# Moving part of the pattern adds of an attention kernel from VectorE to GpSimd

## The chip, the cores and the metric

The kernel runs on one core of a Trainium2 chip. The metric is the device time of one execution in microseconds (us), the median of several runs. Executions of one kernel agree within some 0.3 per cent, apart from a slower state in some executions, at a lower granted TensorE clock (the share of full speed that PE was allowed); comparisons use fast runs alone. The core has five engines that work side by side and wait for each other by semaphores: PE (TensorE, matmuls), ACT (ScalarE, here the exponentials), DVE (VectorE), POOL (GpSimd) and SP, which issues transfers.

## The reference

Self-attention over 2048 positions, width 448, 16 heads of 28, in bf16:

```python
qkv = (x @ wqkv).reshape(B, S, 3, H, Dh).transpose(2, 0, 3, 1, 4)
scores = einsum("bhqd,bhkd->bhqk", q, k) * Dh ** -0.5
o = einsum("bhqk,bhkd->bhqd", softmax(scores), v)
out = o.transpose(0, 2, 1, 3).reshape(B, S, D) @ wo
```

## The kernel before

The 16 units of work (four groups of four heads, four chunks of 512 queries) each have 16 key tiles, so 256 key tiles of four heads. For most tiles ScalarE takes the exponential straight from PSUM, two banks at a time. For the rest, called batches, VectorE makes it another way: it turns a score into an int16 whose bits, read as fp16, approximate the exponential. Three patterns that differ by a constant (0, 341, 683) are used, and PE sums their three products. So a batch costs VectorE four reads of PSUM (one for each head) and two adds in SBUF over all four heads, and PE three passes in place of one:

```python
D_COUNT = (4, 5, 6, 3, 5, 6, 4, 6, 4, 4, 5, 5, 5, 4, 6, 3)   # batches in each unit: 75
TERM_D = (0, 341, 683)
...
r = P.add("dve", ... e.tensor_scalar(PD[:, zs, 0, h * 512:(h + 1) * 512], bank(...), ZBIAS, 0.0, ALU.add, ALU.max) ...)
...                                       # after the fourth head:
h1 = P.add("dve", ... e.tensor_scalar(PD[:, zs, 1, :], PD[:, zs, 0, :], float(TERM_D[1]), None, ALU.add) ...)
h2 = P.add("dve", ... e.tensor_scalar(PD[:, zs, 2, :], PD[:, zs, 0, :], float(TERM_D[2]), None, ALU.add) ...)
```

`P.add` records an operation with an estimate of its duration. A scheduler in the kernel places all of them by these estimates, and what reaches the chip is **one fixed order for each engine**, with semaphores for the true dependencies. Nothing is reordered afterwards: an operation that is late holds all that stands behind it on its engine.

Of the kernel before, what the change touches and what calls it, by code (L numbers as in the profile page):

```python
# [7 lines left out]
ALU = mybir.AluOpType  # L8
# [10 lines left out]
class _Op:  # L19
    __slots__ = ("eng", "emit", "deps", "after", "dur", "prio", "name", "idx", "sig", "count",  # L20
                 "t0", "t1", "dma_group", "dma_index", "acq", "rel", "banks", "slack", "nbytes", "relpool", "acq_slack", "kind", "units", "heads", "ride", "hold", "fill", "lock", "fill_unit")

    def __init__(self, eng, emit, deps, after, dur, prio, name, idx, dma_group):
# [27 lines left out]
        self.lock = False  # L51

# [10 lines left out]
class _Prog:  # L63

    SYNC_LAT = 135.0
    LAT = {"pe": 230.0, "act": 192.0, "dve": 135.0, "pool": 140.0}
# [5 lines left out]
    HOLD_BACK = 540.0  # L72
    BIGLOOK = 150.0
# [28 lines left out]
    def pe_dur(self, prev, op, t):  # L102

        if op.kind is None:
            return op.dur
        one, switch = (430.0, 110.0) if t < self.COLD_UNTIL else (218.0, 100.0)
        if prev is None or prev.kind != op.kind:
            return switch + one * op.units
        if op.kind == "r" and op.heads and not set(op.heads) & self.burst:
            return 60.0  # L110
        return one * op.units

    def schedule(self):
        ops = self.ops
        n = len(ops)
# [18 lines left out]
        def start_of(i, ft):  # L134
# [8 lines left out]
            if op.lock:  # L143
                st = max(st, self.lock_free)
            if op.hold is not None and op.hold.t0 is not None:
# [149 lines left out]
D_COUNT = (4, 5, 6, 3, 5, 6, 4, 6, 4, 4, 5, 5, 5, 4, 6, 3)  # L295
# [38 lines left out]
def _fast(nc, x, wqkv, wo, out, n_heads=16):  # L334
# [35 lines left out]
    with es:  # L370
# [38 lines left out]
        P.pool("M", [4, 5, 6, 7])  # L409
# [135 lines left out]
        def proj_v(g, c, prio):  # L545
# [3 lines left out]
            for j in range(4):  # L549
# [8 lines left out]
                mms.append((f, [dma_x[c], dma_w[(2, 1 if g else 0)]] + wdep(c), "f", 1.1))  # L558
# [6 lines left out]
            for k in range(2):  # L565
# [3 lines left out]
                           deps=[ev, ms_v1], after=[sc], dur=345, prio=g * 4 + c - 2.0, name=f"vb{g}_{c}_{k}")  # L569
                v_ev[(g, c)].append(sc)  # L570
            src = VX[:, xs, :].rearrange("p (n h d) -> p n h d", n=4, d=DH)[:, j0:4:js, :, :]
            for j in range(NTERM):
                dst = VC[:, s0:s0 + nb, j, g * 128:(g + 1) * 128].rearrange("p n (h r) -> p n h r", r=32)[:, :, :, 0:DH]
                sc = P.add("pool", (lambda e, dst=dst, j=j: e.tensor_scalar(dst, src, TERM_C[j], 1.0, ALU.mult, ALU.mult)),  # L574
                           deps=[ev, ms_c1[j]], after=[sc], dur=350, prio=g * 4 + c, name=f"vc{g}_{c}_{j}")
            vc_ev[(g, c)] = sc
# [36 lines left out]
        while i < NA:  # L613
            w = 2
            groups.append(list(range(i, min(i + w, NA))))
            i += w
# [4 lines left out]
        LEAD = 4  # L621
        NMP = 4
        RIDE = 12000.0
# [51 lines left out]
        def out_proj(n, pr, eng):  # L675
# [3 lines left out]
            for gg in range(G):  # L679
                def f_op(e, gg=gg):  # L680
# [3 lines left out]
                            after=[prev], kind="f", units=0.9, prio=pr if gg == 0 else min(pr, -4.0), name=f"OP{n}_{gg}", acq=(("M", 1) if gg == 0 else None), slack=3000.0 if gg == 0 else 0.0)  # L684
# [16 lines left out]
        PRE_LEAD = -0.20  # L701
        s_tail = []
        op_last = []

        def post_unit(u):
# [22 lines left out]
            for k in range(NMP):  # L728
# [3 lines left out]
                           deps=[l4], after=[nm], dur=400, prio=pr + 0.2, name=f"NM{u}_{k}")  # L732
            ots_last[ub] = nm
# [5 lines left out]
        def tail():  # L739
# [7 lines left out]
            b_l, b_p = (0, 2)[nl % 2], (0, 2)[(nl - 1) % 2]  # L747
# [3 lines left out]
            def pbank(j):  # L751
                return heads_[j].banks[0] if j < NQT - 1 else b_p
            for j in range(NQT):
                n = c * NQT + j
                op = None
                for gg in range(G - 1):
                    def f_pre(e, j=j, n=n, gg=gg):
# [3 lines left out]
                    op = P.add("pe", f_pre, deps=[otn_ev[(gg, c)]] + dma_wo[-1:] + ([bank_last[b_p]] if first and j == NQT - 1 else []),  # L761
                               after=([last_s[0]] if first and j == NQT - 1 else sd_of[u][-4:] + op_last[-4:]) if first else [op],
                               kind="f", units=0.9, prio=(NU - PRE_LEAD if gg < 2 else T) + 0.1 * j + 0.01 * gg, name=f"PREOP{j}_{gg}", acq=("M", 1) if first and j < NQT - 1 else None)
# [8 lines left out]
            N1B = (b_p + 1, b_l)  # L772
            N2B = (b_l + 1, b_p + 1)
# [11 lines left out]
            for k in range(2):  # L785
# [14 lines left out]
                for j in (2 * k, 2 * k + 1):  # L800
# [5 lines left out]
                    if j % 2 == 0:  # L806
                        ev = P.add("act", (lambda e, j=j: e.activation(OUTS[:, j, :], bank(pbank(j))[:, 0:D], AF.Identity)), deps=[fin, outs_last[j]], dur=540,
                                   prio=-50.0 + j, name=f"OPEV{n}", rel=[(heads_[j], 0)] if j < NQT - 1 else [])
                    else:
                        ev = P.add("dve", (lambda e, j=j: e.tensor_copy(OUTS[:, j, :], bank(pbank(j))[:, 0:D])), deps=[fin, outs_last[j]], dur=600,  # L810
                                   prio=-50.0 + j, name=f"OPEV{n}", rel=[(heads_[j], 0)] if j < NQT - 1 else [])
# [74 lines left out]
        z_tiles = {}  # L886

# [23 lines left out]
        for gi, gr in enumerate(groups):  # L911
            tl = [a_tiles[a] for a in gr]
            w = len(tl)
            b0 = (0, 2)[gi % 2]
# [15 lines left out]
            s = P.add("pe", f_s, deps=deps, after=[last_s[0]], kind="r", units=1.0, heads=tuple(h for _, _, h in tl), prio=-1000.0 + pos, name=f"S{gi}")  # L930
            last_s[0] = s
            s.hold = last_exp[0]
            while release and release[0][0] - 0.06 <= pos:
                release.pop(0)[1].after.append(s)
            ex = P.add("act", (lambda e, p0=p0, w=w, b0=b0: e.activation(PT[:, p0 * 512:(p0 + w) * 512], bank(b0, w), AF.Exp, scale=ESCALE)),  # L935
                       deps=[s] + [pt_last.get(p0 + j) for j in range(w)], after=[last_exp[0]], dur=51 + w * 427, prio=pos, name=f"E{gi}")
# [9 lines left out]
            for (bi, h) in d_at[gi]:  # L946
# [3 lines left out]
                sd = P.add("pe", (lambda e, hold=hold, u=u, kt=kt, h=h: s_one(e, hold[0].banks[0], u, kt, h)), deps=s_deps(u, kt), after=[s],  # L950
                           kind="r", units=1.0, heads=(h,), prio=-1000.0 + pos + 0.0001, name=f"SD{bi}_{h}", acq=("M", 1))
# [4 lines left out]
                          deps=[sd, z_last[zs][0]], dur=600, prio=-90.0, name=f"R{bi}_{h}", rel=[(sd, 0)])  # L956
                z_tiles.setdefault(bi, []).append(r)
                if len(z_tiles[bi]) == 4:
# [4 lines left out]
                    h2 = P.add("dve", (lambda e, zs=zs: e.tensor_scalar(PD[:, zs, 2, :], PD[:, zs, 0, :], float(TERM_D[2]), None, ALU.add)),  # L963
                               deps=rs_ + [z_last[zs][2]], after=[h1], dur=600, prio=pos, name=f"H{bi}_2")
                    evs += [[h1], [h2]]

                    def mk(u=u, kt=kt, zs=zs, evs=evs):
# [3 lines left out]
                        z_last[zs][0] = op  # L971
# [17 lines left out]
        ckb = (0, 2)[(len(groups) - 1) % 2]  # L989
# [728 lines left out]
```

## Time and profile before

| | before |
|---|---|
| median | 355.8 us |
| span of the profiled run | 353.3 us |
| exponentials on ScalarE | 362, 332.4 us busy, 1.3 us idle before them |
| VectorE busy | 328.9 us |
| GpSimd busy | 68.4 us |

"Busy" is the time in which at least one instruction of an engine was open. Idle time just before a group of instructions is given with the instruction that ended it. The lines are shown in the prediction below.

One more view: GpSimd in the order of time. Columns are the start, the length, the engine, source line, operation, output and input, their forms, and how many followed each other; in brackets the idle time before and its releaser.

```profile
13.35 0.72 POOL L568 TENSOR_SCALAR V<-VX 128x224 bf16<-128x224 f32 x2 [6.26 <-DVE VX L517]
14.03 0.88 POOL L574 TENSOR_SCALAR VC<-VX 128x112 bf16<-128x112 f32 x3
16.09 1.09 POOL L568 TENSOR_SCALAR V<-VX 128x224 bf16<-128x224 f32 x2 [1.18 <-DVE VX L517]
```

The view calls these copies TENSOR_SCALAR.

### The profile page before, as it was taken

The page shows a single profiled execution, that of the slowest core. Times are in us where ns is not written, and L with a number is a line of the kernel's source. Part 1 is how long each engine was busy: PE and PEld are TensorE (multiplying, and loading weights), DVE is VectorE, ACT ScalarE, POOL GpSimd, SP SyncE. Part 2 cuts the span into 40 slices and gives each one's busy share as a digit, 9 for nine tenths or more (in the row PEclk, how much of TensorE's full clock was granted, in tenths as well). Part 3 has the DMA queues.
Part 4 walks back from the last instruction along what each step waited for, and adds up shares of the span by engine and source line. Part 5 has one row for each costly group of instructions (what it writes and reads, how often), then busy time and mean ns, then how long its engine had stood idle before and what let it go on. Part 6 is the DMA issues. An engine that isn't in the chain of part 4 may idle for free.

```text
span 353.3 us, 8533 instructions
## 1 busy us (share of the span) xinstructions
PE 332.5 (94%) x3601; PEld 97.5 (28%) x3601; DVE 328.9 (93%) x557; ACT 335.5 (95%) x367; POOL 68.4 (19%) x157
## 2 busy tenths in 40 slices
PE   7999999999999999999999999999999899999993
PEld 3333232223322222332322222223222222222231
DVE  1788999999999999999999999999999999999962
ACT  2999999999999999999999999999999999999971
POOL 7332030042043013104030121340120301010010
PEclk9999999999999999999999999999999999999999
DMA  9910010010100000010100101010000101020111
GB/s 186 216 24 2 15 39 2 5 32 2 32 19 18 0 5 32 0 34 3 33 2 4 33 1 33 3 33 2 13 21 5 32 30 58 16 71 13 42 34 59
DMA packets 21604, 10.63 MB, mean 30 GB/s; under 512 B 15676, under 2 KB 19516, under 8 KB 21560
## 3 DMA queue, kind: packets, MB, share of 16 engines
q1 hardware_dynamic: 20136, 9.71, 11.4%
q8 instruction: 30, 0.49, 0.6%
q10 hardware_dynamic: 1424, 0.31, 0.5%
q14 instruction: 14, 0.11, 0.1%
HBM read 5.83 MB, written 2.08 MB: 22 GB/s over the span
## 4 chain that ended last, share of the span: by engine, by line
ACT 87%; PE 7%; DVE 2%; DMA 2%; SPq 0%; issue 0%
ACT PT L935 87%; PE ps L846 3%; PE ps L894 2%; DMA xT<-in_x_dram 2%; DVE PD L961 1%; PE ps L758 1%; DVE PD L955 1%; DVE PD L963 1%; SPq L442 0%; PE ps L533 0%; PE ps L804 0%; PE ps L793 0%; PE ps L681 0%; PE ps L780 0%; DVE OUTS L810 0%
## 5 line engine op out<-in xcount | busy, mean ns | idle before, releaser
L935 ACT ACTIVATE PT<-ps 128x1024 bf16<-128x1024 f32 x362 | 332.4, 1252 | 1.3 <-PE ps L894 1.3
L955 DVE TENSOR_SCALAR PD<-ps 128x512 int16<-128x512 f32 x300 | 192.7, 682 | 7.8 <-PE ps L894 6.7
L894 PE MATMUL ps<-QT,KT 28*128 28x512 bf16 x1024 | 148.9, 384 | 11.1 <-ACT PT L935 9.5
L846 PE MATMUL ps<-PD,VC 128*32 128x512 f16 x900 | 80.0, 386 | 0.9 <-DVE PD L963 0.5
L894 PEld LDWEIGHTS ps<-QT,KT 28*128 28x128 bf16 x1024 | 37.9, 91 | 149.7 <-ACT PT L935 141.4
L846 PE MATMUL ps<-PT,V 128*32 128x512 bf16 x724 | 64.5, 385 | 0.7 <-DVE KT L517 0.2
L730 POOL TENSOR_TENSOR QT<-RB,OTS 128x128 bf16<-128x128 f32 x60 | 30.8, 544 | 161.7 <-DMA RB<-scr_r 161.5
L963 DVE TENSOR_SCALAR PD<-PD 128x2048 int16<-128x2048 int16 x75 | 53.5, 713 | 0.0
L961 DVE TENSOR_SCALAR PD<-PD 128x2048 int16<-128x2048 int16 x75 | 53.2, 709 | 0.1
L533 PE MATMUL ps<-xT,w_raw 128*32 128x512 bf16 x512 | 42.6, 385 | 1.4 <-DMA xT<-in_x_dram 0.6
L568 POOL TENSOR_SCALAR V<-VX 128x224 bf16<-128x224 f32 x32 | 12.6, 412 | 113.0 <-DVE VX L517 112.9
L846 PEld LDWEIGHTS ps<-PD,VC 128*32 128x32 bf16 x900 | 19.1, 94 | 32.6 <-issue 22.2
L846 PEld LDWEIGHTS ps<-PT,V 128*32 128x32 bf16 x724 | 15.7, 94 | 23.9 <-issue 20.7
L555 PE MATMUL ps<-w_raw,xT 128*128 128x112 bf16 x256 | 20.8, 215 | 0.0
L574 POOL TENSOR_SCALAR VC<-VX 128x112 bf16<-128x112 f32 (+1 forms) x48 | 19.0, 408 | 1.0
L555 PEld LDWEIGHTS ps<-w_raw,xT 128*128 128x128 bf16 x256 | 13.3, 98 | 10.9 <-issue 9.5
L533 PEld LDWEIGHTS ps<-xT,w_raw 128*32 128x32 bf16 x512 | 10.0, 94 | 19.5 <-issue 13.1
L681 PE MATMUL ps<-wop,QT 128*128 128x448 bf16 x48 | 13.5, 358 | 0.1
L517 DVE CAST KT<-ps 128x512 bf16<-128x512 f32 x16 | 11.0, 686 | 0.4 <-PE ps L533 0.3
L515 DVE TENSOR_SCALAR QT<-ps 128x512 bf16<-128x512 f32 x15 | 10.3, 685 | 0.3 <-PE ps L533 0.2
L713 DVE COPY OTS<-ps 128x512 f32<-128x512 f32 x15 | 10.3, 684 | 0.0
L517 DVE COPY VX<-ps 128x448 f32<-128x448 f32 x16 | 9.9, 618 | 0.3 <-PE ps L555 0.2
(50 smaller groups left out, 50.5 us busy)
## 6 DMA issues: line engine op xcount, KB each, us to landing
RB<-scr_r SPq DMA_DIRECT2D x60, 64.0 KB, 2.0
out_dram<-OUTS SPq DMA_DIRECT2D x16, 112.0 KB, 1.7
w_raw<-in_wqkv_dram SPq DMA_DIRECT2D x3, 249.0 KB, 4.3
wop<-in_wo_dram SPq DMA_DIRECT2D x16, 24.5 KB
w_raw<-in_wqkv_dram ACTq DMA_DIRECT2D x3, 87.0 KB, 3.9
scr_l<-OTS SPq DMA_DIRECT2D x15, 8.0 KB
LT<-scr_l SPq DMA_DIRECT2D x15, 8.0 KB, 1.6
scr_r<-RS SPq DMA_DIRECT2D x15, 8.0 KB, 1.4
```

The costliest lines, as they stand in the source:

```text
L517: fe = (lambda e: e.tensor_copy(evac[0](), evac[1](hold[0].banks[0])))
L533: ins = e.matmul(ps[32 * h:32 * h + 32, b * 512:(b + 1) * 512], w_raw[:, wi(c, it), col:col + 32], xT[:, it, c * 512:(c + 1) * 512], start ...
L555: ins = e.matmul(ps[:, b * 512 + j * GD:b * 512 + (j + 1) * GD], xT[:, it, n * 128:(n + 1) * 128], w_raw[:, wi(c, it), 2 * D + g * GD:2 * ...
L574: sc = P.add("pool", (lambda e, dst=dst, j=j: e.tensor_scalar(dst, src, TERM_C[j], 1.0, ALU.mult, ALU.mult)), deps=[ev, ms_c1[j]], after=[ ...
L681: return e.matmul(bank(hold[0].banks[0])[:, 0:D], QT[:, gg, n * 128:(n + 1) * 128], wop[:, gg, :], start=(gg == 0), stop=(gg == G - 1))
L730: nm = P.add("pool", (lambda e, k=k: e.tensor_tensor(QT[:, g, c * QCH + k * w_:c * QCH + (k + 1) * w_], RB[:, ub, k * w_:(k + 1) * w_], OT ...
L846: return e.matmul(ps[32 * h:32 * h + 32, accb(u) * 512:(accb(u) + 1) * 512], lhsT, rhs, start=first, stop=False, skip_group_check=True, ti ...
L894: return e.matmul(bank(b), KT[32 * h:32 * h + DH, g, kt * 128:(kt + 1) * 128], QT[32 * h:32 * h + DH, g, c * QCH:(c + 1) * QCH], start=Tru ...
L935: ex = P.add("act", (lambda e, p0=p0, w=w, b0=b0: e.activation(PT[:, p0 * 512:(p0 + w) * 512], bank(b0, w), AF.Exp, scale=ESCALE)), deps=[ ...
L955: r = P.add("dve", (lambda e, hold=hold, zs=zs, h=h: e.tensor_scalar(PD[:, zs, 0, h * 512:(h + 1) * 512], bank(hold[0].banks[0]), ZBIAS, 0 ...
L961: h1 = P.add("dve", (lambda e, zs=zs: e.tensor_scalar(PD[:, zs, 1, :], PD[:, zs, 0, :], float(TERM_D[1]), None, ALU.add)), deps=rs_ + [z_l ...
L963: h2 = P.add("dve", (lambda e, zs=zs: e.tensor_scalar(PD[:, zs, 2, :], PD[:, zs, 0, :], float(TERM_D[2]), None, ALU.add)), deps=rs_ + [z_l ...
```

## The change

VectorE and ScalarE both stand near 94 per cent, GpSimd at 19. For 72 per cent of the batches the second add goes to GpSimd, head by head as soon as the head's PSUM read is done. The scheduler is made to treat VectorE's adds in SBUF and GpSimd's work as excluding each other (point (1) of the prediction says why), so it gets a lock between them, and it starts a GpSimd piece together with a PSUM read on VectorE. The freed time is used for three more batches, so six fewer exponentials. The diff, cut to its core:

```diff
-D_COUNT = (4, 5, 6, 3, 5, 6, 4, 6, 4, 4, 5, 5, 5, 4, 6, 3)
+D_COUNT = (5, 4, 6, 6, 5, 4, 4, 4, 5, 5, 5, 5, 6, 5, 5, 4)
...
+            if op.pair and order["dve"]:
+                last = order["dve"][-1]
+                if last.t1 > st and (last.lock or st > last.t0 + self.PAIR_LATE):
+                    st = last.t1 + 1.0
...
-        LEAD = 4
+        LEAD = 18
...
+        POOL_SHARE = 72
+        GDUR = 590
...
+                if on_pool(bi):
+                    gp = z_pool.setdefault(bi, [])
+                    gp.append(P.add("pool", (lambda e, zs=zs, h=h: e.tensor_scalar(PD[:, zs, 2, h * 512:(h + 1) * 512], PD[:, zs, 0, h * 512:(h + 1) * 512],
+                                                                                  float(TERM_D[2]), 0.0, ALU.add, ALU.add)),
+                                    deps=[r, z_last[zs][2]], after=gp[-1:], dur=GDUR, prio=-90.0 + 0.001 * gi, name=f"G{bi}_{h}"))
+                    gp[-1].lock = True
+                    gp[-1].pair = True
```

The scheduler is told 590 ns for a piece (`GDUR`). Latencies, unit times, two more planning constants and the banks of the last unit are adjusted as well, and a PSUM read now waits for all three passes of the batch that had its buffer before (cut here).

More of the change, by code (lines that the diff above doesn't have):

```diff
@@ L20 @@
     __slots__ = ("eng", "emit", "deps", "after", "dur", "prio", "name", "idx", "sig", "count",
-                 "t0", "t1", "dma_group", "dma_index", "acq", "rel", "banks", "slack", "nbytes", "relpool", "acq_slack", "kind", "units", "heads", "ride", "hold", "fill", "lock", "fill_unit")
+                 "t0", "t1", "dma_group", "dma_index", "acq", "rel", "banks", "slack", "nbytes", "relpool", "acq_slack", "kind", "units", "heads", "ride", "hold", "fill", "lock", "pair", "fill_unit")
     def __init__(self, eng, emit, deps, after, dur, prio, name, idx, dma_group):
@@ L51, in __init__ @@
         self.lock = False
+        self.pair = False
 class _DmaGroup:
@@ L65 @@
     SYNC_LAT = 135.0
-    LAT = {"pe": 230.0, "act": 192.0, "dve": 135.0, "pool": 140.0}
+    LAT = {"pe": 225.0, "act": 185.0, "dve": 135.0, "pool": 140.0}
     SAME_LAT = 200.0
@@ L72 @@
     HOLD_BACK = 540.0
+    PAIR_LATE = 250.0
     BIGLOOK = 150.0
@@ L105, in pe_dur @@
             return op.dur
-        one, switch = (430.0, 110.0) if t < self.COLD_UNTIL else (218.0, 100.0)
+        one, switch = (430.0, 110.0) if t < self.COLD_UNTIL else (226.0, 100.0)
         if prev is None or prev.kind != op.kind:
@@ L109, in pe_dur @@
         if op.kind == "r" and op.heads and not set(op.heads) & self.burst:
-            return 60.0
+            return 8.0
         return one * op.units
@@ L407, in i32v @@
             return ap.bitcast(I32)
-        P.pool("M", [4, 5, 6, 7])
+        GW = (2, 2)
+        GB = (0, GW[0])
+        MB = list(range(sum(GW), 8))
+        P.pool("M", MB)
         ms_zw = P.add("pool", lambda e: e.memset(i32v(ZW[:, :]), 0), dur=120, prio=-20, name="ms_zw")
@@ L557, in f @@
                     return ins
-                mms.append((f, [dma_x[c], dma_w[(2, 1 if g else 0)]] + wdep(c), "f", 1.1))
+                mms.append((f, [dma_x[c], dma_w[(2, 1 if g else 0)]] + wdep(c), "f", 0.92))
             xs = vx_n[0] % 3
@@ L569, in proj_v @@
                            deps=[ev, ms_v1], after=[sc], dur=345, prio=g * 4 + c - 2.0, name=f"vb{g}_{c}_{k}")
+                sc.lock = True
                 v_ev[(g, c)].append(sc)
@@ L575, in proj_v @@
                            deps=[ev, ms_c1[j]], after=[sc], dur=350, prio=g * 4 + c, name=f"vc{g}_{c}_{j}")
+                sc.lock = True
             vc_ev[(g, c)] = sc
@@ L613, in _fast @@
         while i < NA:
-            w = 2
+            w = GW[len(groups) % 2]
             groups.append(list(range(i, min(i + w, NA))))
@@ L620, in _fast @@
                 g_of[a] = gi
-        LEAD = 4
+        LEAD = 18
         NMP = 4
-        RIDE = 12000.0
+        RIDE = 6000.0
         d_at = [[] for _ in groups]
@@ L683, in out_proj @@
                 opm = P.add("pe", f_op, deps=[otn_ev[(gg, cc)]] + (([otn_ev[(g_, cc)] for g_ in range(G)] + dma_wo[-1:]) if gg == 0 else []),
-                            after=[prev], kind="f", units=0.9, prio=pr if gg == 0 else min(pr, -4.0), name=f"OP{n}_{gg}", acq=(("M", 1) if gg == 0 else None), slack=3000.0 if gg == 0 else 0.0)
+                            after=[prev], kind="f", units=0.86, prio=pr if gg == 0 else min(pr, -4.0), name=f"OP{n}_{gg}", acq=(("M", 1) if gg == 0 else None), slack=3000.0 if gg == 0 else 0.0)
                 prev = opm
@@ L699, in out_proj @@
                                   nbytes=128 * D * 2)
-        PRE_LEAD = -0.20
+        PRE_LEAD = 0.00
         s_tail = []
+        ck_bank = []
         op_last = []
@@ L732, in post_unit @@
                            deps=[l4], after=[nm], dur=400, prio=pr + 0.2, name=f"NM{u}_{k}")
+                nm.lock = True
             ots_last[ub] = nm
@@ L746, in tail @@
             nl = len(groups) - 1
-            b_l, b_p = (0, 2)[nl % 2], (0, 2)[(nl - 1) % 2]
+            NPM = min(len(MB) - 1, NQT)
+            spare = [GB[(nl - 1) % 2] + i for i in range(GW[(nl - 1) % 2])] + [GB[nl % 2] + i for i in range(GW[nl % 2])]
+            pre_b = [spare.pop(0) for _ in range(NQT - NPM)]
+            N1B = (spare.pop(0), spare.pop(0))
+            N2B = (spare.pop(0), N1B[0])
+            ck_bank.append(N1B[1])
             pre = []
@@ L751, in pbank @@
             def pbank(j):
-                return heads_[j].banks[0] if j < NQT - 1 else b_p
+                return heads_[j].banks[0] if j < NPM else pre_b[j - NPM]
             for j in range(NQT):
@@ L760, in tail @@
                     first = gg == 0
-                    op = P.add("pe", f_pre, deps=[otn_ev[(gg, c)]] + dma_wo[-1:] + ([bank_last[b_p]] if first and j == NQT - 1 else []),
-                               after=([last_s[0]] if first and j == NQT - 1 else sd_of[u][-4:] + op_last[-4:]) if first else [op],
-                               kind="f", units=0.9, prio=(NU - PRE_LEAD if gg < 2 else T) + 0.1 * j + 0.01 * gg, name=f"PREOP{j}_{gg}", acq=("M", 1) if first and j < NQT - 1 else None)
+                    op = P.add("pe", f_pre, deps=[otn_ev[(gg, c)]] + dma_wo[-1:] + ([bank_last[pre_b[j - NPM]]] if first and j >= NPM else []),
+                               after=([last_s[0]] if first and j >= NPM else sd_of[u][-4:] + op_last[-4:]) if first else [op],
+                               kind="f", units=0.86, prio=(NU - PRE_LEAD if gg < 2 else T) + 0.1 * j + 0.01 * gg, name=f"PREOP{j}_{gg}", acq=("M", 1) if first and j < NPM else None)
                     if first:
@@ L771, in tail @@
                                 after=av[-1:], dur=340, prio=-95.0, name=f"ACCEV{u}_{k}"))
-            N1B = (b_p + 1, b_l)
-            N2B = (b_l + 1, b_p + 1)
             rs_h = []
@@ L807, in tail @@
                         ev = P.add("act", (lambda e, j=j: e.activation(OUTS[:, j, :], bank(pbank(j))[:, 0:D], AF.Identity)), deps=[fin, outs_last[j]], dur=540,
-                                   prio=-50.0 + j, name=f"OPEV{n}", rel=[(heads_[j], 0)] if j < NQT - 1 else [])
+                                   prio=-50.0 + j, name=f"OPEV{n}", rel=[(heads_[j], 0)] if j < NPM else [])
                     else:
                         ev = P.add("dve", (lambda e, j=j: e.tensor_copy(OUTS[:, j, :], bank(pbank(j))[:, 0:D])), deps=[fin, outs_last[j]], dur=600,
-                                   prio=-50.0 + j, name=f"OPEV{n}", rel=[(heads_[j], 0)] if j < NQT - 1 else [])
+                                   prio=-50.0 + j, name=f"OPEV{n}", rel=[(heads_[j], 0)] if j < NPM else [])
                     outs_last[j] = P.add("sp", (lambda e, n=n, j=j: e.dma_start(of[n * 128:(n + 1) * 128, :], OUTS[:, j, :])), deps=[ev], after=[outs_last[j]],
@@ L886, in _fast, with on_pool @@
         z_tiles = {}
+        z_pool = {}
+        z_all = [[] for _ in range(NZ)]
+        s_first = {}
+        FREE_SD = False
+        POOL_SHARE = 72
+        GDUR = 590
+        def on_pool(bi):
+            return (bi + 1) * POOL_SHARE // 100 > bi * POOL_SHARE // 100
         def s_deps(u, kt):
@@ L913, in _fast @@
             w = len(tl)
-            b0 = (0, 2)[gi % 2]
+            b0 = GB[gi % 2]
             pos = tl[0][0] + (gr[0] - a_start[tl[0][0]]) / float(a_start[tl[0][0] + 1] - a_start[tl[0][0]])
@@ L929, in f_s @@
                 return ins
-            s = P.add("pe", f_s, deps=deps, after=[last_s[0]], kind="r", units=1.0, heads=tuple(h for _, _, h in tl), prio=-1000.0 + pos, name=f"S{gi}")
+            s = P.add("pe", f_s, deps=deps, after=[last_s[0]], kind="r", units=0.945, heads=tuple(h for _, _, h in tl), prio=-1000.0 + pos, name=f"S{gi}")
             last_s[0] = s
@@ L935, in _fast @@
             ex = P.add("act", (lambda e, p0=p0, w=w, b0=b0: e.activation(PT[:, p0 * 512:(p0 + w) * 512], bank(b0, w), AF.Exp, scale=ESCALE)),
-                       deps=[s] + [pt_last.get(p0 + j) for j in range(w)], after=[last_exp[0]], dur=51 + w * 427, prio=pos, name=f"E{gi}")
+                       deps=[s] + [pt_last.get(p0 + j) for j in range(w)], after=[last_exp[0]], dur=63 + w * 427, prio=pos, name=f"E{gi}")
             last_exp[0] = ex
@@ L949, in _fast @@
                 hold = []
-                sd = P.add("pe", (lambda e, hold=hold, u=u, kt=kt, h=h: s_one(e, hold[0].banks[0], u, kt, h)), deps=s_deps(u, kt), after=[s],
-                           kind="r", units=1.0, heads=(h,), prio=-1000.0 + pos + 0.0001, name=f"SD{bi}_{h}", acq=("M", 1))
+                sd = P.add("pe", (lambda e, hold=hold, u=u, kt=kt, h=h: s_one(e, hold[0].banks[0], u, kt, h)), deps=s_deps(u, kt), after=[s if not FREE_SD else s_first.setdefault(bi, s)] + z_all[zs],
+                           kind="r", units=0.945, heads=(h,), prio=-1000.0 + pos + 0.0001, name=f"SD{bi}_{h}", acq=("M", 1))
                 sd.ride = RIDE
@@ L955, in _fast @@
                 r = P.add("dve", (lambda e, hold=hold, zs=zs, h=h: e.tensor_scalar(PD[:, zs, 0, h * 512:(h + 1) * 512], bank(hold[0].banks[0]), ZBIAS, 0.0, ALU.add, ALU.max)),
-                          deps=[sd, z_last[zs][0]], dur=600, prio=-90.0, name=f"R{bi}_{h}", rel=[(sd, 0)])
+                          deps=[sd] + z_all[zs], dur=600, prio=-90.0, name=f"R{bi}_{h}", rel=[(sd, 0)])
                 z_tiles.setdefault(bi, []).append(r)
+                if on_pool(bi):
[5 more added lines that the diff above has]
+                    gp[-1].pair = True
                 if len(z_tiles[bi]) == 4:
@@ L962, in _fast @@
                                deps=rs_ + [z_last[zs][1]], dur=600, prio=pos, name=f"H{bi}_1")
-                    h2 = P.add("dve", (lambda e, zs=zs: e.tensor_scalar(PD[:, zs, 2, :], PD[:, zs, 0, :], float(TERM_D[2]), None, ALU.add)),
-                               deps=rs_ + [z_last[zs][2]], after=[h1], dur=600, prio=pos, name=f"H{bi}_2")
-                    evs += [[h1], [h2]]
+                    h1.lock = True
+                    if on_pool(bi):
+                        h2 = z_pool.pop(bi)
+                    else:
+                        h2 = [P.add("dve", (lambda e, zs=zs: e.tensor_scalar(PD[:, zs, 2, :], PD[:, zs, 0, :], float(TERM_D[2]), None, ALU.add)),
+                                    deps=rs_ + [z_last[zs][2]], after=[h1], dur=600, prio=pos, name=f"H{bi}_2")]
+                        h2[0].lock = True
+                    evs += [[h1], h2]
                     def mk(u=u, kt=kt, zs=zs, evs=evs):
@@ L970, in mk @@
                             z_last[zs][j] = op
-                        z_last[zs][0] = op
+                        z_all[zs] = [z_last[zs][j] for j in range(NTERM)]
                         unit_done(u, 1)
@@ L987, in _fast @@
         c3 = P.add("dve", (lambda e: e.tensor_reduce(CKM[:, :], CKF[:, :], AX.X, ALU.min)), deps=[c5, c3], dur=80, prio=NU + 5, name="CKM")
-        ckb = (0, 2)[(len(groups) - 1) % 2]
+        ckb = ck_bank[0]
         c4 = P.add("pe", (lambda e: e.matmul(ps[0:1, ckb * 512:ckb * 512 + 1], CKM[:, :], ONE[:, :], start=True, stop=True)),
```

## The prediction

> **What bounds the kernel now.** I read four views in this order: busy time by engine, the costliest groups, the chain that ended last, and then who waited for whom. Busy time first:
>
> ```profile
> PE 332.5 (94%) x3601; PEld 97.5 (28%) x3601; DVE 328.9 (93%) x557; ACT 335.5 (95%) x367; POOL 68.4 (19%) x157
> ```
>
> Three engines stand at 93 to 95 per cent, and GpSimd (POOL) at 19. This row alone doesn't say which of the three sets the end. The groups and the chain do:
>
> ```profile
> ACT 87%; PE 7%; DVE 2%; DMA 2%; SPq 0%; issue 0%
> ...
> L935 ACT ACTIVATE PT<-ps 128x1024 bf16<-128x1024 f32 x362 | 332.4, 1252 | 1.3 <-PE ps L894 1.3
> L955 DVE TENSOR_SCALAR PD<-ps 128x512 int16<-128x512 f32 x300 | 192.7, 682 | 7.8 <-PE ps L894 6.7
> L894 PE MATMUL ps<-QT,KT 28*128 28x512 bf16 x1024 | 148.9, 384 | 11.1 <-ACT PT L935 9.5
> L846 PE MATMUL ps<-PD,VC 128*32 128x512 f16 x900 | 80.0, 386 | 0.9 <-DVE PD L963 0.5
> ...
> L963 DVE TENSOR_SCALAR PD<-PD 128x2048 int16<-128x2048 int16 x75 | 53.5, 713 | 0.0
> L961 DVE TENSOR_SCALAR PD<-PD 128x2048 int16<-128x2048 int16 x75 | 53.2, 709 | 0.1
> ```
>
> The exponentials of ScalarE (362 pieces of two PSUM banks) follow each other for 332.4 us with 1.3 us idle before them in all, and 87 per cent of the chain is this one line. The printed mean of 1252 ns is not the pace: neighbours overlap, and 332.4 / 362 = **0.918 us a piece** is. So ScalarE sets the end. VectorE is close behind (idle before its PSUM reads: 7.8 us), and PE waits for ScalarE. The view of who waited for whom says the last most plainly:
>
> ```profile
> PEld ps L894 <- ACT PT L935: 141.4, 341, 0.5
> ...
> DVE PD L955 <- PE ps L894: 6.7, 19, 1.5
> ...
> ACT PT L935 <- PE ps L894: 1.3, 2, 0.7
> ```
>
> Of 362 score groups, 341 found the weight load of PE waiting for an exponential to free its bank. ScalarE itself waited twice.
>
> Outside the exponentials lie a head and a tail. In the order of time the first one starts at 9.58 us, and the last stretch is
>
> ```profile
> 336.69 5.93 ACT L935 ACTIVATE PT<-ps 128x1024 bf16<-128x1024 f32 x6
> ```
>
> so the last ends at 342.6 and 353.3 - 342.6 = 10.7 us follow (normalisation of the last unit, output matmuls, the output transfer). 9.6 + 333.0 + 10.7 = 353.3.
>
> **What the Trainium skill says.** (1) "SBUF — State Buffer", Who interferes with whom: GpSimd's only port pair is VectorE's second one. A VectorE operation in a mode that uses both ports and a GpSimd operation exclude each other for the whole instruction; a VectorE operation with one input from PSUM doesn't contend. The trace agrees: the pattern adds in SBUF (line 961) take 686 ns at the median, but 1015 ns at most, and two GpSimd copies of 128x224 take 0.72 us at 13.35 us, but 1.09 us at 16.09 us, where such an add ran from 15.93 to 16.61. (2) "VectorE: DVE Perf Modes", The perf-mode tier table: a 16-bit scalar operation on 2048 elements in SBUF runs in 4x mode in 693 ns. The trace has 709 and 713 as means, so these adds are of the kind that locks. (3) "GPSIMD Engine Reference", Elementwise: a body of one or two operations costs 1.03 cycles an element, at 1.2 GHz 0.86 ns. (4) "Perfetto Trace Analysis", GPSIMD Engine Instruction: reported durations there are unreliable, the spacing of starts is to be used. In the trace two copies of 128x224 start at 13.35 and the next group at 14.03, so 0.34 us each. An estimate for the new piece of 128x512 is thus 0.34 + 288 x 0.86 ns = **0.59 us**; no such piece is in the trace before.
>
> **The change part by part.**
>
> *Balance.* The counts of batches on VectorE add up to 75 before and 78 after. With 256 key tiles of four heads this leaves (256 - 78) x 4 = 712 tiles for ScalarE in place of 724, and the instruction order of the built kernel confirms 356 exponentials, 6 fewer. At 0.918 us: **-5.5 us on ScalarE**, on the path.
>
> *VectorE.* 12 more PSUM reads at 192.7 / 300 = 0.642 us: +7.7. 3 more first adds at 0.709: +2.1. Second adds 75 to 22 (56 of 78 batches go to GpSimd), 53 fewer at 0.713: -37.8. Sum **-28.0**, 328.9 to 300.9 us. Nearly all of it is beside the path, because VectorE is not the bound: what it buys is the room to give it three more batches without binding.
>
> *GpSimd.* 56 x 4 = 224 pieces at the estimated 0.59 us: +132 us, on 68.4: about 200 of 348 us. The adds left on VectorE, 78 + 22 = 100 at about 0.69, close the port for 69 us more; 269 of 348 still fits.
>
> *PE.* Three more batches mean nine more passes (four matmuls side by side) with the patterns and three fewer with exponentials: +6. A pass is 0.216 us by the starts (at 30.24, 30.45, 30.67 us in the order of time), so +1.3 us. The dummy matmuls that keep the accumulator busy rise from 24 to 104, 20 passes, +4.3 us, placed where the scheduler sees spare time. Bursts of score matmuls fall from 359 to 351. A burst with the switches into and out of it costs about 0.43 us (0.32 from its start to the next pass, and 0.11 where four passes from 32.40 took until 33.38): -3.4. Sum about **+2 us** on an engine that waits for ScalarE. A period of 0.918 us holds one burst and two passes (0.32 + 0.43 + 0.11 = 0.86), so it fits by 0.06, and three passes overrun by 0.16. In the order of the instructions, gaps with three or more passes rise only from 4 to 9.
>
> *The scheduler's constants* (latencies, unit times, the lead of the VectorE tiles from 4 to 18, the lock and the pairing) move order alone. The order at the end is nearly as before: the same three output matmuls between the last accumulation and the normalisation. I give head and tail no gain.
>
> *Sum.* 9.6 + 356 x 0.918 + 1.3 (the same idle) rounds to a span 5.5 shorter: 353.3 - 5.5 = 347.8. The timed median lies 2.5 above that span, so 355.8 - 5.5 = 350.3. I add 0.2 for waits that GpSimd brings: **350.5 us, 1.5 per cent faster**, which by the 2 per cent mark is "the same".
>
> **The rivals.** (a) *A wait for GpSimd takes the place of VectorE's.* PE runs in order, so a late pattern piece holds the third pass of a batch, behind it the next scores, and then ScalarE. For it: four pieces in a row per batch, none may run while an add of VectorE holds the port, and no semaphore enforces the pairing that the scheduler planned. Against it: from the end of an exponential, scores take about 0.19 + 0.39 = 0.58 us by the starts in the order of time, with 0.918 to do it in, so some 0.3 us of lateness is absorbed, and the lead of 18 tiles gives patterns more time. If each of the 56 batches cost 0.1 us, the gain would be gone: 356; I expect a fraction of it. (b) *The port lock eats VectorE's relief.* A collision that makes each of 100 adds wait half a piece costs 100 x 0.3 = 30 us and puts VectorE back to 331 us. That is below ScalarE's 336 still minus the 5.5, so it would be tight: 351 to 354. Against it: a piece of 0.59 fits beside a PSUM read of 0.642, and in the order the adds now stand in 85 runs rather than one by one. (c) *PE becomes the bound*: 90 per cent by the count above, with too many passes in some gaps: 351 to 352. (d) *More than the exponentials is won*: the 1.3 us of idle vanishes, or the tail shortens by the moved banks: 348 to 349.
>
> **Range and chances.** The floor is the count of exponentials: without any idle, 349.0; beyond that the head or tail must shrink. So low is 348.2. Rivals (a) to (c) give 351 to 354, and I set high at 354.0. Faster by over 2 per cent needs less than 348.7, which needs both all idle gone and some tail: 0.13. Slower by over 2 per cent needs 362.9, an outright failure of the GpSimd path: 0.03. The same: 0.84.
>
> **What would show each step.** Right: exponentials x356 with about 327 us busy at 0.918 and idle before them under 2 us; the chain still over 85 per cent ScalarE; VectorE's busy time about 301 us; GpSimd about 200; pieces spaced at about 0.6 us; the tail after the last exponential 10 to 11 us. Wrong: idle of ScalarE of 4 us or more with releasers in the score matmuls, and before those PE waiting for the GpSimd line (rival a); mean of the SBUF adds on VectorE at 0.9 us or more (b); three-pass gaps ahead of each ScalarE wait (c); a tail under 10 us (d). The prediction as a whole fails if the exponentials' pace itself changes, since every figure rests on 0.918.

## The result

The changed kernel takes **569.2 us** (median of 4 runs, 568.2 to 578.7, the last of these slow and left out of the ratio) against 355.7. The ratio is 1.599, 95 per cent interval 1.596 to 1.602: sixty per cent slower. e3_truecost and e4_share30 below, with the very same GpSimd piece, are correct. Ratios here are the mean time of one kernel's fast runs over that of the other's of the same rounds, so not quite the ratio of the medians quoted.

Busy time by engine of the changed kernel:

```profile
PE 431.2 (76%) x3705; PEld 106.5 (19%) x3705; DVE 326.4 (58%) x519; ACT 350.8 (62%) x361; POOL 500.8 (88%) x381
```

GpSimd went from 68 to 501 us, where I had expected 200. The chain that ended last (the work followed back from the last instruction, at each step to what released it), by engine and by line:

```profile
POOL 56%; PE 34%; issue 4%; DVE 2%; DMA 1%; ACT 1%; SPq 0%; POOLq 0%
POOL PD L986 52%; PE ps L862 13%; PE ps L920 12%; PE ps L542 4%; PE ps L692 2%; DVE PD L981 2%; POOL QT L742 2%; DMA xT<-in_x_dram 1%; POOL VC L584 1%; PE ps L564 1%; ACT PT L961 1%; POOL V L577 1%; PE ps L853 1%; PE ps L776 1%; DVE PD L994 0%
```

ScalarE had 87 per cent of the chain before and has 1 now; the new GpSimd line 986 alone has 52. The costliest groups (busy time, mean ns of one, idle time before and its releaser):

```profile
L986 POOL TENSOR_SCALAR PD<-PD 128x512 int16<-128x512 int16 x224 | 442.5, 2000 | 37.1 <-DVE PD L981 30.5
L961 ACT ACTIVATE PT<-ps 128x1024 bf16<-128x1024 f32 x356 | 347.6, 1038 | 197.6 <-PE ps L920 194.9
L981 DVE TENSOR_SCALAR PD<-ps 128x512 int16<-128x512 f32 x312 | 204.1, 684 | 174.3 <-PE ps L920 172.4
L862 PE MATMUL ps<-PD,VC 128*32 128x512 f16 x936 | 113.1, 506 | 126.3 <-POOL PD L986 113.6
```

A piece on GpSimd takes 442.5 / 224 = **1.98 us** on average, over three times the 0.59 of the plan. Most of the rest is a queue behind it: PE waits 113.6 us before the pattern passes for line 986, ScalarE 194.9 us for the scores that stand behind those passes. The order of time, from 84 to 96 us, shows one such wait whole:

```profile
83.45 0.68 DVE L981 TENSOR_SCALAR PD<-ps 128x512 int16<-128x512 f32 x1
83.49 13.67 POOL L986 TENSOR_SCALAR PD<-PD 128x512 int16<-128x512 int16 x7
...
91.12 0.11 PEld L862 LDWEIGHTS ps<-PD,VC 128*32 128x32 bf16 x4 [8.41 <-POOL PD L986]
91.12 0.62 PE L862 MATMUL ps<-PD,VC 128*32 128x512 f16 x4 [8.11 <-POOL PD L986]
...
92.31 1.02 ACT L961 ACTIVATE PT<-ps 128x1024 bf16<-128x1024 f32 x1 [8.50 <-PE ps L920]
92.35 0.69 DVE L981 TENSOR_SCALAR PD<-ps 128x512 int16<-128x512 f32 x1 [8.22 <-PE ps L920]
```

The seven pieces that start before 96 us run one after the other, 13.67 / 7 = 1.95 us each; PE stops for 8 us, and with it ScalarE and VectorE. From 84.1 to 92.3 us VectorE does nothing at all, so in this stretch no port conflict with it can be what makes the pieces long. The granted TensorE clock fell to 0.715 of full speed (0.999 before), and PE's 3705 matmuls were busy for 431.2 us, where the same matmuls in the same order take 336.0 us at a clock of 0.995 in e8_muladd below. So the lower clock made the loss larger. In the runs that change the piece alone it rises again as the piece gets shorter (0.803, 0.995), so it goes with the slow piece and is no cause apart from it; how much of the loss it makes up was not separated.

### The profile page after: what moved, and what is told of

It is laid out like the page before. It is cut to its first block, busy times and chain, and to the rows that moved or that the text cites. A ratio compares the mean times of both kernels' runs of the same rounds, so it can differ in the third digit from the quotient of the medians.

```text
span 567.5 us, 8964 instructions
## 1 busy us (share of the span) xinstructions
PE 431.2 (76%) x3705; PEld 106.5 (19%) x3705; DVE 326.4 (58%) x519; ACT 350.8 (62%) x361; POOL 500.8 (88%) x381
## 4 chain that ended last, share of the span: by engine, by line
POOL 56%; PE 34%; issue 4%; DVE 2%; DMA 1%; ACT 1%; SPq 0%; POOLq 0%
POOL PD L986 52%; PE ps L862 13%; PE ps L920 12%; PE ps L542 4%; PE ps L692 2%; DVE PD L981 2%; POOL QT L742 2%; DMA xT<-in_x_dram 1%; POOL VC L584 1%; PE ps L564 1%; ACT PT L961 1%; POOL V L577 1%; PE ps L853 1%; PE ps L776 1%; DVE PD L994 0%
## 5 line engine op out<-in xcount | busy, mean ns | idle before, releaser
L986 POOL TENSOR_SCALAR PD<-PD 128x512 int16<-128x512 int16 x224 | 442.5, 2000 | 37.1 <-DVE PD L981 30.5
L961 ACT ACTIVATE PT<-ps 128x1024 bf16<-128x1024 f32 x356 | 347.6, 1038 | 197.6 <-PE ps L920 194.9
L981 DVE TENSOR_SCALAR PD<-ps 128x512 int16<-128x512 f32 x312 | 204.1, 684 | 174.3 <-PE ps L920 172.4
L862 PE MATMUL ps<-PD,VC 128*32 128x512 f16 x936 | 113.1, 506 | 126.3 <-POOL PD L986 113.6
L920 PE MATMUL ps<-QT,KT 28*128 28x512 bf16 x1024 | 183.2, 483 | 2.0 <-ACT PT L961 1.0
L862 PE MATMUL ps<-PT,V 128*32 128x512 bf16 x712 | 85.3, 495 | 0.0
L994 DVE TENSOR_SCALAR PD<-PD 128x2048 int16<-128x2048 int16 x78 | 62.9, 823 | 0.0
L542 PE MATMUL ps<-xT,w_raw 128*32 128x512 bf16 x512 | 52.6, 478 | 0.9 <-DMA xT<-in_x_dram 0.9
L742 POOL TENSOR_TENSOR QT<-RB,OTS 128x128 bf16<-128x128 f32 x60 | 26.5, 467 | 0.1
L564 PEld LDWEIGHTS ps<-w_raw,xT 128*128 128x128 bf16 x256 | 17.1, 116 | 11.5 <-issue 10.6
L1000 DVE TENSOR_SCALAR PD<-PD 128x2048 int16<-128x2048 int16 x22 | 18.2, 826 | 0.0
```

The source lines that it names most:

```text
L542: ins = e.matmul(ps[32 * h:32 * h + 32, b * 512:(b + 1) * 512], w_raw[:, wi(c, it), col:col + 32], xT[:, it, c * 512:(c + 1) * 512], start ...
L564: ins = e.matmul(ps[:, b * 512 + j * GD:b * 512 + (j + 1) * GD], xT[:, it, n * 128:(n + 1) * 128], w_raw[:, wi(c, it), 2 * D + g * GD:2 * ...
L742: nm = P.add("pool", (lambda e, k=k: e.tensor_tensor(QT[:, g, c * QCH + k * w_:c * QCH + (k + 1) * w_], RB[:, ub, k * w_:(k + 1) * w_], OT ...
L862: return e.matmul(ps[32 * h:32 * h + 32, accb(u) * 512:(accb(u) + 1) * 512], lhsT, rhs, start=first, stop=False, skip_group_check=True, ti ...
L920: return e.matmul(bank(b), KT[32 * h:32 * h + DH, g, kt * 128:(kt + 1) * 128], QT[32 * h:32 * h + DH, g, c * QCH:(c + 1) * QCH], start=Tru ...
L961: ex = P.add("act", (lambda e, p0=p0, w=w, b0=b0: e.activation(PT[:, p0 * 512:(p0 + w) * 512], bank(b0, w), AF.Exp, scale=ESCALE)), deps=[ ...
```

## The experiments

Theory A: the piece itself takes 1.9 us on GpSimd, and it is a matter of how it is written. Theory B: the port lock with VectorE makes it long. Theory C: another part of the change (order, lead, pairing) costs time.

### m1_forms: the piece by itself

A separate kernel runs eight pieces of each form on 128x512 elements, spaced without waits, VectorE idle; its output is zeros.

```diff
+e.tensor_scalar(out, in, 683.0, 0.0, ALU.add, ALU.add)     # int16; also in bf16, f32, fp16, int32, mixed
+e.tensor_scalar(out, in, 683.0, None, ALU.add)
+e.tensor_scalar(out, in, 1.0, 1.0, ALU.mult, ALU.mult)      # f32 to bf16, and int16
+e.tensor_tensor(out_i32, in_i32, constant_column, ALU.add)  # two int16 in one int32, 128x256
```

> A measuring kernel; its output is zeros, wrong on purpose. Eight GpSimd pieces of each form follow each other with VectorE idle. Theory A (the integer 16-bit add itself is slow on GpSimd): the change's own piece, 128x512 int16 to int16, is spaced at 1.9 us alone, and the same work in bf16 or f32 at 0.5 to 0.7 us. Theory B (the port lock makes it slow): alone it is spaced at about 0.6 us, beside VectorE's PSUM reads too, and at 1.2 us or more beside VectorE's SBUF adds. Two int16 patterns in one int32, added as 128x256 with a second tensor: 0.6 to 0.8 us under A, if the integer path is cheap there.

GpSimd in the order of time; in turn int16 add and add, one add, bf16 add and add, f32 add and add, f32 to bf16 with two multiplications, int16 with two multiplications, the packed add, and the first form again, first beside PSUM reads of VectorE, then beside its SBUF adds:

```profile
1.84 15.14 POOL L47 TENSOR_SCALAR GO<-A 128x512 int16<-128x512 int16 x8
17.06 11.68 POOL L50 TENSOR_SCALAR GO<-A 128x512 int16<-128x512 int16 x8
28.83 15.15 POOL L53 TENSOR_SCALAR GO<-A 128x512 bf16<-128x512 bf16 x8
44.06 15.14 POOL L56 TENSOR_SCALAR GO<-A 128x512 f32<-128x512 f32 x8
59.29 4.71 POOL L59 TENSOR_SCALAR GO<-A 128x512 bf16<-128x512 f32 x8
64.08 4.70 POOL L62 TENSOR_SCALAR GO<-A 128x512 int16<-128x512 int16 x8
...
109.85 4.60 POOL L77 TENSOR_TENSOR GO<-A,B 128x256 int32<-128x256 int32 x8
...
144.99 15.14 POOL L86 TENSOR_SCALAR GO<-A 128x512 int16<-128x512 int16 x8
160.21 20.02 POOL L90 TENSOR_SCALAR GO<-A 128x512 int16<-128x512 int16 x8
```

Divided by eight: add and add 1.89 us, one add 1.46, two multiplications 0.59, the packed add 0.575. My theory A named the wrong property: the type makes no difference at all (15.14 or 15.15 us in every one), **the operations do**. The packed add with a full second tensor in place of the column takes 0.685 us, within the 0.6 to 0.8 expected. Beside PSUM reads the piece keeps 1.89 us, beside SBUF adds (which run for 17.4 of the 20.0 us) it rises to 2.50: the two do hold each other up, but theory B has little left to explain, since the piece is slow alone.

### m2_forms: which operations

> A second measuring kernel, wrong on purpose. The first one showed add, add at 1.89 us, one add at 1.46 and mult, mult at 0.59 us for the same 128x512, whatever the type. Theory M (a quick path is taken when the first operation is a multiplication): mult then add 0.59, add then mult 1.9. Theory MM (only multiplications alone): mult then add 1.9 too. Mult alone 0.59 or less under both. Beside VectorE's PSUM reads the quick pieces keep 0.59 (no port conflict); beside VectorE's SBUF adds they alternate with them, 1.2 us or more.

```diff
+e.tensor_scalar(out, in, 1.0, 683.0, ALU.mult, ALU.add)    # L48, then the reverse L51
+e.tensor_scalar(out, in, 1.0, None, ALU.mult)              # L54; L57 max, max; L60 subtract alone
+...                                                        # L66 mult, mult and L69 add, add at 128x1024; L78, L85 mult, mult beside VectorE
```

```profile
1.84 4.70 POOL L48 TENSOR_SCALAR GO<-A 128x512 int16<-128x512 int16 x8
6.62 4.70 POOL L51 TENSOR_SCALAR GO<-A 128x512 int16<-128x512 int16 x8
11.41 11.69 POOL L54 TENSOR_SCALAR GO<-A 128x512 int16<-128x512 int16 x8
23.18 15.10 POOL L57 TENSOR_SCALAR GO<-A 128x512 int16<-128x512 int16 x8
38.36 11.68 POOL L60 TENSOR_SCALAR GO<-A 128x512 int16<-128x512 int16 x8
...
52.35 8.12 POOL L66 TENSOR_SCALAR GO<-A 128x1024 int16<-128x1024 int16 x8
60.55 28.81 POOL L69 TENSOR_SCALAR GO<-A 128x1024 int16<-128x1024 int16 x8
...
103.98 9.36 POOL L78 TENSOR_SCALAR GO<-A 128x512 int16<-128x512 int16 x16
...
123.40 16.36 POOL L85 TENSOR_SCALAR GO<-A 128x512 int16<-128x512 int16 x16 [0.81 <-DVE RO L97]
```

Multiply then add takes 4.70 / 8 = 0.59 us, which theory MM denied, and so does add then multiply, which theory M denied. One multiplication alone takes 1.46, against what both theories said, a subtraction alone 1.46 too, and max with max 1.89. Neither theory held. In these runs the pairs of two operations with at least one multiplication that were tried are quick (mult and mult, mult and add, add and mult); the pairs tried without one (add and add, max and max) and the single operations tried (add, subtract, multiply) are slow. The slope from 512 to 1024 elements is (8.12 - 4.70) / 8 / 512 = 0.83 ns an element for the quick pair and (28.81 - 15.14) / 8 / 512 = 3.3 ns for the slow one. Why the hardware or its program does so, no run tells. Beside PSUM reads the quick piece stays at 9.36 / 16 = 0.585 us, beside SBUF adds it needs 1.02, less than the 1.2 expected.

### e5_oneadd, e6_mulmul, e7_packed, e8_muladd: the same order, only the piece rewritten

In all four the instructions of every engine stand in the order of the changed kernel (compared instruction by instruction; e7_packed has one small memset more at the start). Only the piece differs; its lines are shortened here.

```diff
-... float(TERM_D[2]), 0.0, ALU.add, ALU.add)
+... float(TERM_D[2]), None, ALU.add)                                # e5_oneadd
+... 1.0, 1.0, ALU.mult, ALU.mult)                                   # e6_mulmul, no add: wrong on purpose
+... e.tensor_tensor(PD as int32, PD as int32, constant column 683 * 65537, ALU.add)   # e7_packed
+... 1.0, float(TERM_D[2]), ALU.mult, ALU.add)                       # e8_muladd
```

> The changed kernel, instruction for instruction in the same order, with the second addition of zero left out of the GpSimd piece: 1.46 in place of 1.89 us by the first measuring kernel. If the piece's duration is the cause, GpSimd loses 224 x 0.43 = 96 us and the time falls by nearly as much, to 460 to 490 us. If the order or the port is the cause: little change, over 540 us. Result stays correct.

> The same order, the piece multiplies by 1 twice (0.59 us by the first measuring kernel) and does not add: wrong numbers on purpose. If the piece's duration is the whole cause, the prediction's own assumption now holds: 348 to 354 us. If the order, the lead or the pairing costs something besides, 356 to 370 us.

> The same order, and a correct piece: two int16 patterns are taken as one int32 and a constant column is added with a second input (0.575 us by the first measuring kernel). Duration theory: 348 to 354 us, correct. If two inputs on GpSimd conflict more with VectorE than one, 355 to 365 us.

> The changed kernel in the same order, the piece written as a multiplication by 1 and then the addition: 0.59 us in the second measuring kernel. Correct. Duration theory: the same as the packed piece, 351.5 to 353 us.

| kernel | piece alone | busy time of the 224 pieces | time | clock | result |
|---|---|---|---|---|---|
| the change | 1.89 us | 442.5 us | 569.2 us | 0.715 | no check |
| e5_oneadd (1 run) | 1.46 us | 351.8 us | 487.8 us | 0.803 | correct |
| e6_mulmul (1 run) | 0.59 us | 147.8 us | 352.6 us | 0.995 | wrong on purpose |
| e7_packed | 0.575 us | 145.9 us | 352.3 us | 0.995 | correct |
| e8_muladd | 0.59 us | 147.5 us | 352.6 us | 0.995 | correct |

With order, lead, pairing and all other engines' work the same, the time follows the piece. From the change to e5_oneadd GpSimd's pieces lose 90.7 us of busy time and the kernel 81.4 us; at 0.59 us the whole loss is gone, and the clock is back. Theory A holds in its corrected form, and as all else is unchanged, theory C is out as a cause of the loss. Against the kernel before of the same rounds e8_muladd has the ratio 0.9916 (0.9903 to 0.9929) and e7_packed 0.9910 (0.9893 to 0.9927): **0.8 to 0.9 per cent faster than before**, and correct. By the 2 per cent mark that is "the same", but both intervals lie below 1; which of the two is better is not shown. e5_oneadd landed within the range given for it (460 to 490). The profile of e8_muladd, busy time, then chain by engine, then groups:

```profile
PE 336.0 (96%) x3705; PEld 99.5 (28%) x3705; DVE 312.7 (89%) x519; ACT 331.7 (95%) x361; POOL 213.8 (61%) x381
...
PE 46%; ACT 45%; DVE 5%; DMA 2%; issue 0%; SPq 0%
```

```profile
L961 ACT ACTIVATE PT<-ps 128x1024 bf16<-128x1024 f32 x356 | 328.5, 1156 | 2.1 <-PE ps L920 1.5
...
L986 POOL TENSOR_SCALAR PD<-PD 128x512 int16<-128x512 int16 x224 | 147.5, 674 | 96.7 <-DVE PD L981 88.7 <-PE ps L862 4.5 <-PE ps L920 2.2
L862 PE MATMUL ps<-PD,VC 128*32 128x512 f16 x936 | 82.7, 384 | 1.3 <-DVE PD L994 0.7 <-DVE PD L1000 0.3 <-POOL PD L986 0.2
...
L994 DVE TENSOR_SCALAR PD<-PD 128x2048 int16<-128x2048 int16 x78 | 57.7, 755 | 0.0
...
L1000 DVE TENSOR_SCALAR PD<-PD 128x2048 int16<-128x2048 int16 x22 | 16.7, 760 | 0.0
```

GpSimd now waits 96.7 us for work and is off the path: PE's wait for it before the pattern passes is 0.2 us, where it was 113.6. ScalarE is back, sharing the chain with PE.

### e2_share0: the rest of the change without GpSimd

```diff
-        POOL_SHARE = 72
+        POOL_SHARE = 0
```

> The changed kernel with no batch on GpSimd, all else of the change kept (78 batches, constants, lead). Theory A and B alike: VectorE has 300.9 + 56 x 0.713 = 340.8 us of work and is near its bound; 352 to 358 us. If another part of the change (order, lead, pairing) is to blame, it stays far above 360.

It took 367.5 us, ratio 1.037 (1.031 to 1.043), correct: a miss by some 10 us. ScalarE was not the loser:

```profile
L961 ACT ACTIVATE PT<-ps 128x1024 bf16<-128x1024 f32 x356 | 328.3, 1146 | 4.1 <-PE ps L920 1.8
```

Its last exponential ends at 341.4 us, earlier than before (342.6), but 23.7 us follow to the end, not 10.7. In that stretch VectorE is busy 18.35 of 20 us (340 to 360), still with batches. From 334.6 to 351.6 us the chain runs on VectorE's instructions, but for 0.6 us. So at 339.9 us of work in all, VectorE sets the end in this plan: the three more batches pay only when GpSimd takes adds off it. (The order differs too, so this run alone doesn't clear the rest of the change; the four runs above do.)

### e11_count75: GpSimd without the three more batches

```diff
 (on e8_muladd)
-D_COUNT = (5, 4, 6, 6, 5, 4, 4, 4, 5, 5, 5, 5, 6, 5, 5, 4)
+D_COUNT = (4, 5, 6, 3, 5, 6, 4, 6, 4, 4, 5, 5, 5, 4, 6, 3)
```

> As e8_muladd, with the batch counts of the kernel before (75, so 362 exponentials). If the gain comes from the six fewer exponentials: 355 to 358 us, no faster than before. If relief of VectorE alone helps: 352 to 354 us.

355.5 us, ratio 0.9996 (0.9983 to 1.0009): the same as the kernel before, although VectorE's busy time fell from 328.9 to 303.6 us:

```profile
PE 338.9 (96%) x3693; PEld 99.6 (28%) x3693; DVE 303.6 (86%) x503; ACT 336.2 (95%) x367; POOL 205.5 (58%) x373
```

Relief of VectorE brings no gain here until it is spent on fewer exponentials. The run carries the other parts of the change too (PE is busy 6.4 us longer than in the kernel before), so a small gain that they ate can't be ruled out.

### e10_nopair: without the planner's lock and pairing

```diff
 (on e8_muladd)
-                    gp[-1].lock = True
-                    gp[-1].pair = True
-                    (and every other .lock = True)
```

> As e8_muladd, with the scheduler's lock and pairing rules left out (GpSimd pieces and SBUF adds are planned freely; the order changes). If the rules matter: more port conflicts, SBUF adds on VectorE at a mean over 0.8 us (0.76 with the rules), 354 to 360 us. If not: within 1 us of e8.

357.1 us, ratio 1.0016 (0.9999 to 1.0033) to before, so about 1 per cent slower than e8_muladd and within the range:

```profile
L958 ACT ACTIVATE PT<-ps 128x1024 bf16<-128x1024 f32 x356 | 329.8, 1159 | 6.3 <-PE ps L917 5.5
...
L989 DVE TENSOR_SCALAR PD<-PD 128x2048 int16<-128x2048 int16 x78 | 59.9, 780 | 0.1
...
L994 DVE TENSOR_SCALAR PD<-PD 128x2048 int16<-128x2048 int16 x22 | 19.3, 876 | 0.0
```

The first adds rose from 755 to 780 ns and the second adds from 760 to 876; over all 100 of them the mean went from 756 to 801 ns, just at the 0.8 us that I had named, and the GpSimd pieces from 674 to 711 ns. So there are more conflicts, as expected. ScalarE's idle went from 2.1 to 6.3 us, and VectorE's share of the chain from 5 to 30 per cent. Without the rules the whole gain of the change is gone; how much of that is by conflicts and how much by the changed order is not shown.

### e9_nofill: without the dummy matmuls

```diff
 (on e8_muladd, in the function that adds dummy matmuls)
-    TICK, ONE, WANT = 3413.0, 213.0, 0.55
+    TICK, ONE, WANT = 3413.0, 213.0, 0.0
```

> As e8_muladd, without the 104 dummy matmuls that keep PE's accumulator busy (26 passes, about 5.6 us of PE). If PE now shares the bound (the chain of the packed piece's run is 46 per cent PE), 350 to 351.5 us; if they sit in time that PE waits anyway, the same as e8 within 0.5 us; if PE's clock drops for want of them, slower.

353.6 us, ratio 0.9927 (0.9908 to 0.9946), beside 0.9916 for e8_muladd: the intervals overlap, so no effect is shown either way. PE's busy time fell by 4.9 us and no gain is seen, which fits dummies that sit in time that PE waits anyway. Two of the six runs were slow.

### e3_truecost and e4_share30: telling the scheduler the true cost

```diff
-        GDUR = 590
+        GDUR = 1950        # both; e4_share30 also POOL_SHARE = 30
```

> The scheduler is told 1950 ns for a GpSimd piece in place of 590; 72 per cent stay on GpSimd. Theory A1 (throughput: GpSimd simply has too much work): 224 x 1.95 + 60 = about 500 us of GpSimd work, so 510 to 530 us however well it is ordered. Theory A2 (mostly the wrong plan: PE waits in order at places planned too early): well under 480 us.

> The scheduler is told 1950 ns, and 30 per cent of the batches go to GpSimd: 23 batches, 92 pieces, 179 us there beside 60 of other work; VectorE about 324 us. Theory A1: GpSimd fits, so 350 to 356 us. If a long piece hurts VectorE's SBUF adds through the port lock (92 pieces open a window of 1.9 us each), 356 to 370 us.

Both were misses. With 72 per cent and the true cost the time was 642.1 us (1 run), worse than with the false one; with 30 per cent 431.1 us, ratio 1.214, though GpSimd was busy only 254.5 of 428 us. In e3_truecost one group stands out:

```profile
L853 PE MATMUL ps<-ZM,ZW 128*32 128x512 bf16 x3292 | 244.8, 393 | 0.0
```

The planner saw long waits and put 3292 dummy matmuls into them (728 in e4_share30, 104 in the change). These two runs therefore mix two things, and they don't tell how good a plan with the slow piece could be. That stays open. What they do show is that a true estimate alone repairs nothing here: the slow form must go.

## Why the prediction was wrong

The range was 348.2 to 354.0 us and the time 569.2. By its own steps:

- **What bounds the kernel now** was right: in e11_count75 VectorE's relief alone moves nothing, and e8_muladd, with six exponentials fewer, is faster. One reading was slightly off: 0.68 of the 1.3 us idle lies before the first exponential, so the sum counts it twice, in the idle and in the 9.6 us of the head, and the floor of 349.0 "without any idle" is some 0.7 us too low.
- **The step that failed** is the cost of the piece: "An estimate for the new piece of 128x512 is thus 0.34 + 288 x 0.86 ns = 0.59 us". It measured 1.89 us alone and 1.98 in the kernel. The estimate took its base from copies that multiply twice and its slope from the skill's line on bodies of one or two operations, and applied both to a piece that adds twice. The text said itself that no such piece was in the trace before, then went on as if one were, and left 0.03 for a clear loss. The scheduler's own 590 ns agreed, which looked like support; it is no measurement, and it equals what two multiplications, or a multiplication and an add, take.
- So "269 of 348 still fits" failed: the pieces alone were 442.5 us busy, and GpSimd 500.8 in all.
- **Rival (a)**, a wait for GpSimd in place of VectorE's, was the right mechanism: PE in order, scores behind the late pass, ScalarE behind the scores. It was sized at up to 0.1 us a batch because the piece was held to be short. The sign to look for ("before those PE waiting for the GpSimd line") is there, 113.6 us.
- **Rival (b)**, the port lock, is real but small with a quick piece: the first adds on VectorE average 755 ns in e8_muladd against 709 before. (The row of the skill's table that the prediction used for these adds names bf16; that int16 adds hold GpSimd up as well is what m1_forms and m2_forms show.) VectorE was busy 312.7 us, not 300.9. About 3 us of that difference are the two groups of SBUF adds (57.7 + 16.7 = 74.4 us, 71.0 expected). The rest is the prediction's bookkeeping: neighbouring instructions overlap in the trace, and it took busy times of groups off a busy time in which an overlap counts once. Added up, the groups of VectorE exceed its busy time by some 29 us before and by some 20 in e8_muladd.
- With a piece that costs what the prediction assumed (0.59 us alone, 147.5 / 224 = 0.66 in the kernel), the kernel takes 352.6 us: inside the range, 2.1 above the point, and "the same" by the 2 per cent mark. The span fell by 2.6 us, not 5.5. Of the 2.9 us difference 1.6 are the pace, 328.5 / 356 = 0.923 in place of 0.918 us; 0.8 the idle before exponentials (2.1 against 1.3); 0.2 a first exponential at 9.8 in place of 9.58; 0.3 the tail, 11.0 in place of 10.7. The "pace" is a mean, though, and the exponential itself got no slower: by the starts in the kept traces, the median distance from one to the next is 904 ns in e8_muladd and 914 before, but 38 of 355 distances are over 0.95 us, where 14 of 361 were. By the same traces ScalarE waited for scores there, and PE has 46 per cent of this kernel's chain and 7 of the one before. That points to rival (c), but its own sign is missing, since 33 of the 38 have two passes ahead of their scores and not three; what made PE late each time is not shown. GpSimd was hardly it (matmuls of the pattern passes waited 0.2 us for it, their weight loads 1.7), and e9_nofill, without the dummy matmuls, was no faster.

## What to carry to other kernels

Before work is moved to an engine, look up or measure the very instruction there, with its operations and not only its shape and type: a number from a neighbouring form is a guess, and a constant in a scheduler is one too. On an engine with a fixed order a piece that is late stops everything behind it, so its cost has to be known before its place is planned. And where two engines are both nearly full, relief of the one that doesn't set the end pays only when it is turned into less work for the one that does.

## What the Trainium skill lacked or had wrong

- "GPSIMD Engine Reference", Elementwise — side-by-side cycle accounting, gives 1.03 cycles an element for bodies of one or two operations. The runs agree for two multiplications (0.83 ns an element, 1.0 cycle at its 1.2 GHz; a multiplication and an add take the same 0.59 us at 512 elements), but two adds take 3.3 ns (4.0 cycles by that clock), so 1.89 against 0.59 us for 128x512; a single add, subtraction or multiplication takes 1.46 us. What the page lacks is that the operations decide and not the type.
- The same page, Engine selection, calls one-input work on GpSimd "roughly line-rate". Of the `tensor_scalar` forms tried, that holds for the quick pairs alone; the slow forms take 2.5 to 3.2 times as long at 128x512.
- No page that I read says that two int16 values can be added on GpSimd as one int32 with a constant column: 0.575 us for 128x512 values (e7_packed), on top of the exact integer add that "GPSIMD Engine Reference", Engine selection, describes.
- "SBUF — State Buffer", Who interferes with whom, was right: the quick piece takes 0.585 us beside PSUM reads of VectorE and 1.02 beside its SBUF adds.
